# Loads in order of need, and batch 1's attention between group 0's products

## The chip, the core and the metric

The kernel runs on one core of a Trainium2 chip. The metric is the device time of one execution in microseconds (us). All times come from the timed runs of the kernel before and from one profiled execution of it.

## The reference

Sliding-window causal attention (8 batches, 8 heads, 576 positions of 64 values, a window of 64), whose output goes as 4608 tokens of 512 values through a multiplicative feed-forward part:

```python
scores = q @ k.T / 8                     # per batch and head
scores = where(0 <= i - j < 64, scores, -1e9)
attn   = softmax(scores) @ v             # -> x [4608, 512]
h      = ((x @ w1) * (x @ w2)) @ w3      # w1, w2 [512, 1024], w3 [1024, 1024]
out    = h @ w_out                       # w_out [1024, 512], out [4608, 512]
```

## The kernel before

The two last weights are folded once on the chip: `wc = w3 @ w_out` (1024 x 512), in eight parts. `fold_t(fc)` transposes a part of w3 on TensorE and copies it to SBUF, `fold_mm(fc)` multiplies it with w_out, and `fold_step` does the next transposes and one product.

**Attention.** For each batch, `load_qk` brings K and Q in fp32 (1.18 MB each) into a tile `stage`, with positions on partitions; they are cast to fp16 (`cast_third`, a third of the columns at a time, or `cast_qk`, one head of each pair at a time), transposed on TensorE in three groups of six (`transposes(b, which, c)`, with copies out of PSUM into `kT` and `qT`), and then there are six steps `d` per batch (three bands of 192 positions, two halves of the heads). `scores(d)` has TensorE multiply, ACT take the exponential into `pt` (line 279), and POOL mask it (`affine_select`, lines 288 and 290). `values(d)` has TensorE multiply `pt` with V into `o_ps` (line 309), of which there is a single buffer; V carries a block of ones, so that row sums come with it. ACT takes logarithm and exponential of the sums (318, 319, 321), and DVE multiplies (324, 325) into `xT`, the transposed input of the feed-forward part. `load_v` brings a block of V (cast by the DMA), `copy_v` fills the overlaps. `load_qk` may have a gate: a one-column memset on an engine, so that the transfer starts only when that engine's queue has come to this place.

**Feed-forward.** The 4608 tokens are nine groups of 512. `ffn_ab(g, fc)`, a product below, does x @ w1 and x @ w2 for 128 of the 1024 columns (eight matmuls on TensorE, line 395), ACT copies one (400), DVE multiplies (401). `ffn_o(g, t)`, an output product below, multiplies 128 tokens by `wc` (408), DVE copies (410), and `store` sends them out. Group g can start when the attention has filled its 512 columns: group 0 needs batch 0, group 1 needs batch 1's six steps.

**Order.** The kernel sets its order by hand: each engine runs its instructions in the order in which the program writes them, in its own queue. DMAs are issued from the queue of SP (K, Q, stores) and of POOL (V and weights), and an issue is an instruction of that queue, behind everything that stands ahead of it; a queue's ninth transfer waits until its first has landed, and so on. The program is: prologue (batch 0's K and Q, with `keep_busy` matmuls on TensorE that have no use but to be run), six steps of batch 0 with the folds, eight products of group 0, six steps of batch 1 with output products, and from group 1 on a list of `slots` (each a product or an output product) between which `tick(u)` puts the attention of batch 2 and later, by the due times in the loop at the end and the table `late`. `todo` adds batch 2's transposes behind group 1's first slots.

Of the kernel before, what the change touches and what calls it, by code (L numbers as in the profile page):

```python
# [15 lines left out]
P = 128  # L16
# [128 lines left out]
def kernel(  # L145
# [11 lines left out]
    nc = tc.nc  # L157
# [44 lines left out]
    def load_qk(b, which, gate=None):  # L202
        src = k if which == "k" else q
        t = sb.tile([P, 2, TI * D], FP32, name="stage", bufs=4)
        if gate is not None:
            gate(t[:, 0, 0:1], 0.0)
        for j in range(NJ):
            nc.sync.dma_start(out=t[j:P:NJ],
                              in_=src[b, 2 * j:2 * j + 2].rearrange("h (p r) d -> p h (r d)", r=TI))
        raws[which, b] = t  # L210
# [16 lines left out]
    def load_v(b, c):  # L227

        vh = v16s[b % 2].rearrange("p c j (a e) -> p c (j a) e", a=2)[:, :, :, 0:D]
        lo = D if c == 4 else 0  # L230
        s0 = VBLK[c] + lo
        nc.gpsimd.dma_start(out=vh[lo:P, c], in_=v[b, :, s0:s0 + P - lo, :].rearrange("h s d -> s h d"))  # L232

    def copy_v(b, c):
        vh = v16s[b % 2].rearrange("p c j (a e) -> p c (j a) e", a=2)[:, :, :, 0:D]
# [91 lines left out]
    def keep_sums(n):  # L327
# [155 lines left out]
    load_wo()  # L483
    load_w3(0)
    load_w3(1)
# [33 lines left out]
    keep_busy(60)  # L519
# [5 lines left out]
    keep_busy(15)  # L525
# [4 lines left out]
    tps = spare(ps_s, "s_ps")  # L530
    transposes(0, "q", 2, tps[0])
# [68 lines left out]
    for g in range(1, NG):  # L600
# [4 lines left out]
        first = 5 if g == 1 else 0  # L605
# [60 lines left out]
```

## Time and profile before

| | |
|---|---|
| Time, median of 3 runs | 350.1 us (349.34 to 351.72) |
| Profiled execution | 347.68 us, of which the span is 345.9 us |
| Mean granted TensorE clock | 0.918 |
| Busy: TensorE matmul / weight load | 288.4 us (83%) / 168.4 us (49%) |
| Busy: DVE / ACT / POOL | 198.1 us (57%) / 180.2 us (52%) / 178.0 us (51%) |
| Moved by DMA | 38.89 MB, mean 112 GB/s |
| Chain that ended last | TensorE 59%, of it line 395 32% and line 408 16% of the span |

In the profile PE is TensorE's matmuls, PEld its weight loads, DVE the vector engine, ACT the scalar engine, POOL GpSimd, SP the engine that only issues transfers. A row of the timeline gives the start, the time (from the first to the last of its instructions when it holds several), the engine and line, the operation with its tiles, how many, and in brackets the idle time just before with what ended it. Matmuls overlap one another, so a matmul's own duration is longer than its share of the time. A row of a table by stages gives the stretch, and in it the busy time of PE, PEld, DVE, ACT and POOL, the granted clock, the DMA share and the GB/s moved.

### The profile page before, as it was taken

What the parts mean: (1) busy time and instruction counts of PE and PEld (TensorE: products, weight loads), DVE (VectorE), ACT (ScalarE), POOL (GpSimd) and SP (SyncE); (2) the same over time, 40 slices, a digit from 0 to 9 for tenths busy, and PEclk for the clock granted to TensorE, in tenths of its full rate; (3) what the DMA queues carried; (4) which work ended last, traced back from release to release, by engine and by line L of the source; (5) the groups of instructions that cost most, each with busy time, mean ns of one, the idle gap of its engine ahead of it and who ended that gap; (6) DMA issues with size and microseconds to landing.
All of it is one profiled execution on the core that took longest, in us unless ns stands there. A gap on an engine that the chain in (4) does not pass through costs nothing.

```text
span 345.9 us, 5523 instructions
## 1 busy us (share of the span) xinstructions
PE 288.4 (83%) x2007; PEld 168.4 (49%) x2007; DVE 198.1 (57%) x305; ACT 180.2 (52%) x298; POOL 178.0 (51%) x211
## 2 busy tenths in 40 slices
PE   6486955497674977999999999999999999998790
PEld 6363522144332445555555559855555555443230
DVE  4373651156334385677787776757877765554440
ACT  1243741423654244687877876549768866613100
POOL 9258620500759126988887785468776444300000
PEclk9589999599766696999999999999999999999896
DMA  7999706840467950768768767574049011020021
GB/s 161 286 184 203 117 0 224 100 24 0 144 221 152 283 216 0 74 124 270 49 114 270 78 90 235 117 118 63 2 80 114 0 63 61 2 91 33 2 95 39
DMA packets 52182, 38.89 MB, mean 112 GB/s; under 512 B 39296, under 2 KB 42368, under 8 KB 52144
## 3 DMA queue, kind: packets, MB, share of 16 engines
q0 software_dynamic: 41744, 9.96, 31.1%
q1 hardware_dynamic: 10400, 28.47, 23.8%
q8 instruction: 18, 0.29, 0.4%
q14 instruction: 20, 0.16, 0.2%
HBM read 38.80 MB, written 9.44 MB: 139 GB/s over the span
## 4 chain that ended last, share of the span: by engine, by line
PE 59%; DVE 2%; ACT 2%; issue 1%; POOL 1%; DVEq 0%; POOLq 0%; ACTq 0%
PE f_ps L395 32%; PE f_ps L408 16%; PE o_ps L309 4%; PE s_ps L274 4%; PE tp L251 3%; DVE qT L260 1%; ACT qT L260 0%; DVE xT L325 0%; ACT r L321 0%; POOL pt L290 0%; POOL pt L288 0%; ACT ln_s L319 0%; DVE okv L464 0%; DVE chk L461 0%; ACT pt L279 0%
## 5 line engine op out<-in xcount | busy, mean ns | idle before, releaser
L395 PE MATMUL f_ps<-xT,w_sb 128*128 128x512 f16 (+1 forms) x640 | 142.3, 373 | 10.4 <-ACT a_sb L400 8.4
L288 POOL TENSOR_SCALAR_AFFINE_SELECT pt<-pt 128x512 f16<-128x512 f16 (+1 forms) x64 | 52.7, 823 | 82.5 <-ACT pt L279 82.4
L395 PEld LDWEIGHTS <-w_sb 128*128 128x128 f16 x640 | 62.3, 101 | 67.0 <-issue 21.5
L401 DVE TENSOR_TENSOR ab<-f_ps,a_sb 128x512 f16<-128x512 f32 x72 | 49.7, 691 | 35.9 <-PE f_ps L395 26.7
L408 PE MATMUL f_ps<-wc_sb,ab 128*128 128x512 f16 x288 | 69.7, 390 | 0.1
L400 ACT COPY a_sb<-f_ps 128x512 f32<-128x512 f32 x72 | 41.6, 579 | 44.9 <-PE f_ps L395 44.5
L324 DVE TENSOR_TENSOR xT<-o_ps,r 64x384 f16<-64x384 f32 x48 | 26.4, 550 | 57.1 <-ACT r L321 57.1
L279 ACT ACTIVATE pt<-s_ps 128x1024 f16<-128x1024 f32 (+1 forms) x48 | 45.6, 950 | 25.2 <-PE s_ps L274 24.2
L290 POOL TENSOR_SCALAR_AFFINE_SELECT pt<-pt 128x512 f16<-128x512 f16 (+1 forms) x64 | 52.6, 821 | 4.4
L318 ACT ACTIVATE ln_s<-o_ps 64x384 f32<-64x384 f32 x48 | 23.4, 487 | 46.2 <-PE o_ps L309 46.1
L309 PE MATMUL o_ps<-pt,v 128*128 128x128 f16 (+1 forms) x384 | 29.5, 221 | 16.5 <-DVE xT L325 11.8
L408 PEld LDWEIGHTS <-ab 128*128 128x128 f16 x288 | 27.7, 100 | 29.5 <-issue 3.1
L309 PEld LDWEIGHTS <-v 128*128 128x128 f16 x384 | 24.9, 101 | 28.7 <-issue 13.0
L232 POOL DMA_DIRECT2D v<-in_v_dram x40 | 34.4, 867 | 7.0 <-DMA ab<-in_moe_w_out_dram 6.7
L410 DVE COPY t2k<-f_ps 128x512 f32<-128x512 f32 x36 | 24.9, 692 | 12.0 <-PE f_ps L408 11.3
L274 PE MATMUL s_ps<-qT,kT 128*128 128x256 f16 x192 | 28.7, 275 | 3.2 <-DVE qT L260 2.6
L325 DVE TENSOR_TENSOR xT<-o_ps,r 64x384 f16<-64x384 f32 x48 | 26.9, 561 | 0.7
L321 ACT ACTIVATE r<-ln_s 128x384 f32<-128x384 f32 x48 | 25.1, 522 | 1.5
L274 PEld LDWEIGHTS <-kT 128*128 128x128 f16 x192 | 18.2, 101 | 12.9 <-issue 4.0
L260 DVE COPY qT<-tp 64x768 f16<-64x768 f16 x20 | 19.2, 960 | 7.8 <-ACT qT L260 7.6
L319 ACT ACTIVATE ln_s<-o_ps 64x384 f32<-64x384 f32 x48 | 23.2, 482 | 0.6
L255 DVE COPY kT<-tp 128x768 f16<-128x768 f16 x21 | 19.9, 950 | 2.1 <-PE tp L251 2.0
(60 smaller groups left out, 196.3 us busy)
## 6 DMA issues: line engine op xcount, KB each, us to landing
stage<-in_k_dram SPq DMA_DIRECT2D x32, 288.0 KB
stage<-in_q_dram SPq DMA_DIRECT2D x32, 288.0 KB
out_dram<-t2k SPq DMA_DIRECT2D x36, 256.0 KB
v<-in_v_dram POOLq DMA_DIRECT2D x32, 128.0 KB, 4.2
w_sb<-in_moe_w_dram POOLq DMA_DIRECT2D x4, 512.0 KB, 12.9
ab<-in_moe_w_out_dram POOLq DMA_DIRECT2D x1, 1024.0 KB, 15.4
ab<-in_moe_w_dram POOLq DMA_DIRECT2D x2, 512.0 KB, 17.8
xT<-in_moe_w_dram POOLq DMA_DIRECT2D x2, 512.0 KB, 14.4
```

The source lines that it names most:

```text
L232: nc.gpsimd.dma_start(out=vh[lo:P, c], in_=v[b, :, s0:s0 + P - lo, :].rearrange("h s d -> s h d"))
L274: nc.tensor.matmul(s_ps[:, jj, c0:c0 + 2 * n].rearrange("k (a n) -> k a n", a=2), kT[:, 2 * jp + jj, k0:k0 + P], qT[:, 2 * jp + jj, :, q0: ...
L279: nc.scalar.activation(pt[:, :, 0:w], s_ps[:, :, 0:w], AF.Exp, bias=-SHIFT, scale=scale)
L288: nc.gpsimd.affine_select(out=sl, in_=sl, pattern=pat, compare_op=ALU.is_ge, fill=0.0, base=off, channel_multiplier=-1)
L290: nc.gpsimd.affine_select(out=sl, in_=sl, pattern=[[-s, m] for s, m in pat], compare_op=ALU.is_ge, fill=0.0, base=63 - off, channel_multip ...
L309: nc.tensor.matmul(o_ps[:, jj, o0:o0 + n], v16[:, si * 2 + bi, j0 + jj, a * D:a * D + P], pt[:, jj, c0 + a * n:c0 + a * n + n], start=firs ...
L324: nc.vector.tensor_tensor(xs[0:D], o_ps[0:D, :, 0:192], r[0:D], ALU.mult)
L325: nc.vector.tensor_tensor(xs[D:P], o_ps[D:P, :, 192:384], r[D:P], ALU.mult)
L395: nc.tensor.matmul(d[:, f * n + c0:f * n + c1], w[:, dc, (fc + f) * P:(fc + f + 1) * P], xT[:, dc, xc:xc + c1 - c0], start=first, stop=(dc ...
L400: act_cp(a_sb[:, 0:nf * n], a_ps[:, 0:nf * n])
L401: nc.vector.tensor_tensor(ab[:, fc:fc + nf, lo:hi], b_ps[:, 0:nf * n].rearrange("p (f n) -> p f n", f=nf), a_sb[:, 0:nf * n].rearrange("p ...
L408: nc.tensor.matmul(o_ps, ab[:, fc, t * P:t * P + P], wc_sb[:, fc, :], start=(fc == 0), stop=(fc == 7))
```

## The change

K and Q of a batch come in two transfers each (one per head of a pair, 128 partitions) instead of four (32 partitions). In the prologue POOL first clears V's ones, then issues w_out and the first quarter of w3, three V blocks, the rest of w3; the last two V blocks come behind, and the halves of w1 and w2 later, between batch 0's steps, as do V, K and Q of batch 1. The folds are spread over batch 0's six steps, with `scores` two steps ahead instead of one. Group 0's products are spread: three ahead of batch 1's first scores, one more before its second, one in each of the steps 6 to 9; output products stand in and behind the steps 10 and 11. Batch 2's K is transposed between group 0's last output products instead of in `todo`. In `late` V's five blocks come in two bunches.

```diff
     def load_qk(b, which, gate=None):
...
-        for j in range(NJ):
-            nc.sync.dma_start(out=t[j:P:NJ],
-                              in_=src[b, 2 * j:2 * j + 2].rearrange("h (p r) d -> p h (r d)", r=TI))
+        for hh in range(2):
+            nc.sync.dma_start(out=t[:, hh], in_=src[b, hh:H:2].rearrange("j (p r) d -> p j (r d)", r=TI))
...
     late = {0: [("t", 1, "k", 0), ("cast", 1, "q", 0)], 1: [("cast", 1, "q", 1)],
-            2: [("t", 1, "k", 1), ("load", 2, "k")], 3: [("v", 1, 0)],
-            4: [("t", 1, "k", 2), ("v", 1, 2)], 5: [("load", 2, "q"), ("v", 1, 3)],
-            6: [("t", 1, "q", 0), ("v", 1, 4)], 7: [("v", 1, 5), ("cast", 2, "k", 0)],
-            8: [("t", 1, "q", 1)], 9: [("copy", 1, 1), ("cast", 2, "k", 1)],
-            10: [("t", 1, "q", 2)], 11: [("copy", 1, 4)]}
+            2: [("t", 1, "k", 1), ("load", 2, "k")], 4: [("t", 1, "k", 2), ("v", 1, 0, 2, 3)],
+            5: [("load", 2, "q")], 6: [("t", 1, "q", 0), ("v", 1, 4, 5)], 7: [("cast", 2, "k", 0)],
+            8: [("t", 1, "q", 1), ("copy", 1, 4)], 9: [("copy", 1, 1), ("cast", 2, "k", 1)], 10: [("t", 1, "q", 2)]}
...
-    load_wo()
-    load_w3(0)
-    load_w3(1)
...
     ones_of(0)
-    for c in (0, 2, 3):
-        load_v(0, c)
-    load_w3(2)
-    for c in (4, 5):
-        load_v(0, c)
-    load_w3(3)
-    for half in range(2):
-        for i in range(2):
-            load_w12(i, half)
+    load_wo()
+    load_w3(0)
+    load_v(0, 0, 2, 3)
+    for n in range(1, 4):
+        load_w3(n)
     ones_of(1)
+    load_v(0, 4, 5)
...
-    keep_busy(60)
+    keep_busy(75)
...
-    keep_busy(15)
+    keep_busy(10)
...
     keep_busy(10)
+    scores(0)
+    keep_busy(10)
+    scores(1)
+    for i in range(2):
+        load_w12(i, 0)
     w3Ts[0] = fold_t(0)
-    scores(0)
-    w3Ts[1] = fold_t(1)
+    fold_step(0)
+    fold_mm(1, w3Ts.pop(1), dve_cp)
     copy_v(0, 1)
-    fold_mm(0, w3Ts.pop(0), dve_cp)
     for d in range(6):
-        if d < 5:
-            scores(d + 1)
+        if d == 0:
+            w3Ts[2] = fold_t(2)
+        values(d)
+        if d < 4:
+            scores(d + 2)
+        fold_step(d + 2)
+        if d == 0:
+            load_v(1, 0, 2)
+        if d == 1:
+            load_v(1, 3)
+            load_qk(1, "k", nc.vector.memset)
+            load_qk(1, "q")
+        if d == 2:
+            copy_v(0, 4)
+            for i in range(2):
+                load_w12(i, 1)
         if d == 3:
-            copy_v(0, 4)
-        if d < 5:
-            fold_step(d + 1)
-        values(d)
-    fold_step(6)
-    load_qk(1, "k", nc.vector.memset)
-    load_qk(1, "q")
-    fold_step(7)
+            load_v(1, 4)
+        if d == 4:
+            cast_qk(1, "k", 0, dve_cp)
+            cast_qk(1, "k", 1, dve_cp)
+            cast_qk(1, "q", 0, pool_cp)
+            transposes(1, "k", 0)
+    cast_qk(1, "q", 1, dve_cp)
...
-    for c in range(3):
-        cast_third(1, "k", c, act_cp if c != 1 else dve_cp)
-    for c in range(3):
-        cast_third(1, "q", c, act_cp if c != 1 else pool_cp)
-    for c in (0, 2, 3, 4, 5):
-        load_v(1, c)
-    for fc in range(8):
-        ffn_ab(0, fc)
-        if fc in (4, 5, 6):
-            transposes(1, "k", fc - 4)
+    transposes(1, "k", 1)
+    ffn_ab(0, 0)
+    transposes(1, "k", 2)
+    ffn_ab(0, 1)
     tps = spare(ps_v, "o_ps")
     for c in range(3):
         transposes(1, "q", c, tps[c] if c < 2 else None)
+    ffn_ab(0, 2)
+    load_v(1, 5)
+    scores(6)
     copy_v(1, 1)
-    ffn_o(0, 0)
-    scores(6)
...
-    ffn_o(0, 1)
+    ffn_ab(0, 3)
     scores(7)
...
     for d in range(6, 12):
         values(d)
         if d < 10:
             scores(d + 2)
-        if d in (7, 9):
-            ffn_o(0, (d - 3) // 2)
+            ffn_ab(0, d - 2)
+        else:
+            ffn_o(0, d - 10)
             store()
...
+    transposes(2, "k", 0)
+    ffn_o(0, 2)
+    store()
+    transposes(2, "k", 1)
+    ffn_o(0, 3)
+    store()
+    transposes(2, "k", 2)
...
-        first = 5 if g == 1 else 0
+        first = 3 if g == 1 else 0
...
-    todo = {0: [lambda: transposes(2, "k", 0)], 1: [lambda: transposes(2, "k", 1)],
-            2: [lambda: transposes(2, "k", 2), lambda: copy_v(2, 1), lambda: cast_qk(3, "k", 0, pool_cp)],
-            3: [lambda: transposes(2, "q", 0), lambda: cast_qk(3, "k", 1, pool_cp)],
-            4: [lambda: transposes(2, "q", 1), lambda: copy_v(2, 4)], 5: [lambda: transposes(2, "q", 2)]}
+    todo = {0: [lambda: transposes(2, "q", 0), lambda: copy_v(2, 1)],
+            1: [lambda: transposes(2, "q", 1), lambda: copy_v(2, 4), lambda: cast_qk(3, "k", 0, pool_cp)],
+            2: [lambda: transposes(2, "q", 2), lambda: cast_qk(3, "k", 1, pool_cp)]}
```

POOL's queue in the prologue, before (the line numbers are those of each kernel; `ab` holds w_out and half of w3, `xT` the other half for the time of the folds, `w_sb` w1 and w2, `v_0` V of even batches, `v_1` of odd ones):

```order
L433 DMA ab<-in_moe_w_out_dram 128x8x512
L439 DMA ab<-in_moe_w_dram 128x2x1024 x2
L491 MEMSET v_0_85 128x48x64
L232 DMA v_0_85<-in_v_dram 128x8x64 x3
L439 DMA xT<-in_moe_w_dram 128x2x1024
L232 DMA v_0_85<-in_v_dram 64x8x64
L232 DMA v_0_85<-in_v_dram 128x8x64
L439 DMA xT<-in_moe_w_dram 128x2x1024
L429 DMA w_sb<-in_moe_w_dram 128x4x512 x4
L491 MEMSET v_1_86 128x48x64
L288 AFFINE_SELECT pt<-pt 128x2x256
```

The same place after the change, up to the first mask:

```order
L489 MEMSET v_0_85 128x48x64
L434 DMA ab<-in_moe_w_out_dram 128x8x512
L440 DMA ab<-in_moe_w_dram 128x2x1024
L235 DMA v_0_85<-in_v_dram 128x8x64 x3
L440 DMA ab<-in_moe_w_dram 128x2x1024
L440 DMA xT<-in_moe_w_dram 128x2x1024 x2
L489 MEMSET v_1_86 128x48x64
L235 DMA v_0_85<-in_v_dram 64x8x64
L235 DMA v_0_85<-in_v_dram 128x8x64
L291 AFFINE_SELECT pt<-pt 128x2x256
```

The four w1 and w2 transfers have left the place ahead of the first mask, the first memset stands ahead of w_out, and three V blocks stand ahead of all of w3 but its first quarter.

DVE's queue at the end of batch 0's steps, before (`xT` rows are the multiplications of a values step, `k16` and `q16` the casts of batch 1):

```order
L324 TENSOR_TENSOR xT_83<-o_ps_532,r_544 64x2x192
L325 TENSOR_TENSOR xT_83<-o_ps_532,r_544 64x2x192
L324 TENSOR_TENSOR xT_83<-o_ps_548,r_559 64x2x192
L325 TENSOR_TENSOR xT_83<-o_ps_548,r_559 64x2x192
L448 COPY t2k_572<-f_ps_563 128x1024
L455 CAST wc_sb_61<-f_ps_574 128x512
L206 MEMSET stage_584 128x1
L224 CAST k16_608<-stage_584 128x2x6x64
L401 TENSOR_TENSOR ab_621<-f_ps_623,a_sb_632 128x512
```

And after the change, from the multiplications of step 4 on:

```order
L327 TENSOR_TENSOR xT_83<-o_ps_560,r_572 64x2x192
L328 TENSOR_TENSOR xT_83<-o_ps_560,r_572 64x2x192
L449 COPY t2k_585<-f_ps_576 128x1024
L456 CAST wc_sb_61<-f_ps_587 128x512
L216 CAST k16_597<-stage_458 128x18x64 x2
L258 COPY kT_602<-tp_603 128x128x6
L327 TENSOR_TENSOR xT_83<-o_ps_611,r_622 64x2x192
L328 TENSOR_TENSOR xT_83<-o_ps_611,r_622 64x2x192
L216 CAST q16_600<-stage_462 128x18x64
L258 COPY kT_602<-tp_640 128x128x6
L402 TENSOR_TENSOR ab_648<-f_ps_650,a_sb_659 128x512
```

Two wide casts of batch 1's K and a copy of its transposes now stand between the multiplications of step 4 and step 5, and the gate of its load (the memset) has moved out of this place, to step 1.

ACT's queue from the last fold on, before (`a_sb` is the copy of a product, `pt` the exponential of a scores step):

```order
L455 CAST wc_sb_61<-f_ps_595 128x512
L224 CAST k16_608<-stage_584 128x2x6x64 x2
L224 CAST q16_612<-stage_590 128x2x6x64 x2
L400 COPY a_sb_632<-f_ps_622 128x512
L400 COPY a_sb_645<-f_ps_635 128x512
```

And after the change, from the row behind that fold on:

```order
L401 COPY a_sb_659<-f_ps_649 128x512
L401 COPY a_sb_680<-f_ps_670 128x512
L263 COPY qT_1_88<-o_ps_683 64x4x32x6 x2
L263 COPY qT_1_88<-tp_700 64x4x32x6
L401 COPY a_sb_719<-f_ps_709 128x512
L282 ACTIVATE pt_728<-s_ps_723 128x2x384
L401 COPY a_sb_746<-f_ps_736 128x512
L282 ACTIVATE pt_754<-s_ps_749 128x2x384
L321 ACTIVATE ln_s_769<-o_ps_760 64x384
L322 ACTIVATE ln_s_769<-o_ps_760 64x384
L324 ACTIVATE r_772<-ln_s_769 128x384
L282 ACTIVATE pt_781<-s_ps_776 128x1024
```

The casts of batch 1 are gone from ACT's queue, and the copies of the products stand between the scores and values of batch 1 instead of all ahead of them.

More of the change, by code (lines that the diff above doesn't have):

```diff
@@ L225, in cast_third, with v_heads, load_v @@
            t[:, :, 6 * c * D:6 * c * D + 6 * D].rearrange("p hh (i d) -> p hh i d", d=D))
[L227 to L232, printed above, removed]
+    def v_heads(b):
+        return v16s[b % 2].rearrange("p c j (a e) -> p c (j a) e", a=2)[:, :, :, 0:D]
+    def load_v(b, *blocks):
+        vh = v_heads(b)
+        for c in blocks:
+            lo = D if c == 4 else 0
+            s0 = VBLK[c] + lo
+            nc.gpsimd.dma_start(out=vh[lo:P, c], in_=v[b, :, s0:s0 + P - lo, :].rearrange("h s d -> s h d"))
     def copy_v(b, c):
-        vh = v16s[b % 2].rearrange("p c j (a e) -> p c (j a) e", a=2)[:, :, :, 0:D]
+        vh = v_heads(b)
         dve_cp(vh[0:D, c], vh[D:P, c - 1])
@@ L580 @@
             scores(d + 2)
-        if d in (7, 9):
-            ffn_o(0, (d - 3) // 2)
+            ffn_ab(0, d - 2)
+        else:
+            ffn_o(0, d - 10)
             store()
-        if d in (8, 9):
-            cast_qk(2, "k", d - 8, pool_cp)
-            load_v(2, (d - 8) * 2)
+        if d == 7:
+            copy_v(1, 4)
+            load_qk(2, "k", nc.gpsimd.memset)
+            load_qk(2, "q")
+            load_v(2, 0, 2, 3)
+        if d == 9:
+            load_v(2, 4, 5)
+    cast_qk(2, "k", 0, pool_cp)
+    cast_qk(2, "k", 1, pool_cp)
+    transposes(2, "k", 0)
[5 more added lines that the diff above has]
+    transposes(2, "k", 2)
     cast_qk(2, "q", 0, pool_cp)
```

13 lines of the change are left out of this document (1 added, 12 removed).

## The prediction

> **What bounds the kernel now.** I read the page's 40 slices first, then busy time by stage, then the timeline of the first 135 us engine by engine, where each row ends with the idle time before it and what ended it.
>
> ```profile
> PE   6486955497674977999999999999999999998790
> PEclk9589999599766696999999999999999999999896
> 160.00:310.00 150.00, 149.95 (x1099) 89.96 (x1098) 105.05 (x164) 103.49 (x176) 93.33 (x109) 1.00 0.48 94
> ```
>
> A slice is 8.65 us. From slice 18 on TensorE is full, and the stage row says the same: 149.95 of 150 us busy at clock 1.00 between 160 and 310 us. The change leaves that work there, so nothing is to be won in it; its new order of V loads only has to keep it fed. The time to win lies before about 135 us, where the PE digits are 4 to 9 and the granted clock falls to 5 to 7 tenths. That part runs in four stages, and I take a marker for each: V0 (the second half of batch 0's first values step), S (group 0's first product), N (group 1's first product), T (batch 2's first scores). After T both kernels have the same work left, but for two products of 1.73 us.
>
> **Stage 1, start to V0.** The rows of the load and of POOL's queue:
>
> ```profile
> 0.81 2.74 SPq L208 DMA_DIRECT2D stage<-in_k_dram  x4
> 12.14 0.83 ACT L224 CAST k<-stage 128x768 f16<-128x768 f32 x1 [10.05 <-DMA stage<-in_k_dram]
> 16.69 0.83 ACT L224 CAST q<-stage 128x768 f16<-128x768 f32 x1 [0.39 <-DMA stage<-in_q_dram]
> 17.23 1.27 POOL L232 DMA_DIRECT2D v<-in_v_dram  x1 [6.67 <-DMA ab<-in_moe_w_out_dram]
> 19.70 0.70 POOL L439 DMA_DIRECT2D xT<-in_moe_w_dram  x1 [1.20 <-DMA ab<-in_moe_w_dram]
> 22.19 0.78 POOL L429 DMA_DIRECT2D w_sb<-in_moe_w_dram  x1 [1.80 <-DMA ab<-in_moe_w_dram]
> 23.66 2.34 POOL L429 DMA_DIRECT2D w_sb<-in_moe_w_dram  x3 [0.69 <-DMA v<-in_v_dram]
> 22.20 0.49 PE L274 MATMUL s_ps<-qT,kT 128*128 128x256 f16 x4
> 25.98 2.68 POOL L491 MEMSET v<- 128x3072 f16 x1
> 30.87 0.44 PE L309 MATMUL o_ps<-pt,v 128*128 128x64 f16 x7 [0.65 <-POOL pt L290]
> 54.00:62.00 8.00, 2.69 (x13) 1.10 (x12) 0.56 (x1) 2.15 (x3) 0.00 (x0) 0.89 0.88 296
> ```
>
> K is there at 12.1 and Q at 16.7 us, because w_out and w3 flow beside them; the last row (54 to 62 us, batch 1's K and Q with nothing beside them) shows 296 GB/s, the last column. Scores follow Q by 5.5 us (22.20). Then the masks of L288 and L290 wait for POOL, which first waits for landings, issues four w1/w2 transfers and clears v (25.98 to 28.66). V0 is 30.87.
>
> After the change, K (1.18 MB at 296 GB/s: 4.0 us) starts at about 2.2, where data begins today, and is usable at 7.7 with 1.5 us for its end to be seen. POOL clears v first (2.7 us), so w_out's data starts near 6 and shares with Q; Q comes at 12 to 15, scores at 18 to 20. From 6 us on, 1.26 MB of K and Q and 1.05 MB of w_out are left: 7.8 us at 296 GB/s, so w_out lands at 14 to 17 (17.2 today, less at most what K has gained). Behind it in POOL's queue, by the distances between the landings above: w3's first quarter 2.5 us (17.2 to 19.7), V about 1.5 a block for three (22.2 to 23.7, 3.5 in all as they overlap), w3's second quarter 2.5. That quarter is there at 22.5 to 25.5, and its transposes stand ahead of values(0) on TensorE. POOL is free earlier: its last wait is for w3's first quarter, 17 to 19.5, then 0.9 for an issue and 2.1 for the first masks. **V0 falls from 30.87 to about 25.0**: 5.9 us. The longer warm-up (75 matmuls for 60) runs while K is awaited, at 5.5 us per 60 it ends at 8.3, 0.6 after K at most.
>
> **Stage 2, V0 to S.**
>
> ```profile
> 34.19 0.50 PE L309 MATMUL o_ps<-pt,v 128*128 128x128 f16 x8 [0.27 <-DVE xT L325]
> 48.08 0.61 PE L309 MATMUL o_ps<-pt,v 128*128 128x128 f16 x8 [2.88 <-DVE xT L325]
> 53.94 2.75 PE L395 MATMUL f_ps<-xT,w_sb 128*128 128x512 f16 x12
> 17.00 1.02 DVE L224 CAST q<-stage 128x768 f16<-128x768 f32 x2
> 103.06 1.13 POOL L217 CAST k<-stage 128x1152 f16<-128x1152 f32 x1
> ```
>
> A values step waits for DVE to empty its PSUM tile: 30.87 to 34.19 is 3.3 us, five steps to 48.08 are 17.2. I take 3.4 a step. Today S is 53.94, 23.1 us after V0, with the last two folds behind the loop. After, the folds are inside the loop, but batch 1's K is cast on DVE ahead of its transposes, and these stand ahead of values(5). The wide cast on DVE is not in the trace: at least one of the two narrow ones (0.5), at most POOL's 1.13; I take 0.8, nearer to DVE's own row (1.5 times the columns). Two are 1.6. DVE gets to them at V0 + 18.6 (43.6, after values(4)'s multiplications, a copy and a cast), so values(5) comes at 45.7, its multiplications end 3.3 later: **S = 49.0**, 4.9 us earlier than 53.94, if K is there by 43.6 and Q by 49.
>
> Is it? Their gate on DVE opens in step 1 after its multiplications, at V0 + 7.7 = 32.7.
>
> ```profile
> 52.79 2.53 SPq L208 DMA_DIRECT2D stage<-in_k_dram  x4
> 59.93 1.56 ACT L224 CAST k<-stage 128x768 f16<-128x768 f32 x2 [5.21 <-DMA stage<-in_k_dram]
> 63.03 1.56 ACT L224 CAST q<-stage 128x768 f16<-128x768 f32 x2 [1.53 <-DMA stage<-in_q_dram]
> 65.13 5.28 PE L395 MATMUL f_ps<-xT,w_sb 128*128 128x512 f16 x12 [8.44 <-ACT a_sb L400]
> ```
>
> Today K comes 7.1 and Q 10.2 us after the first issue: 39.8 and 42.9 if alone. Beside them run the first halves of w1 and w2, three V blocks and then the second halves. At half the rate (4.0 more for each) they come at 43.8 and 50.9: at most 0.2 us late for K and 1.9 for Q. I count none and keep the 2 us in the range. [...]
>
> **Stage 3, S to N.** Here is the main gain. ACT's in-order queue holds the casts of batch 1 ahead of the copies of the products, and TensorE stands 8.44 us (above) before it goes on at half clock.
>
> ```profile
> 79.97 0.50 PE L251 MATMUL o_ps<-ident,q 128*128 128x128 f16 x6
> 85.61 0.49 PE L274 MATMUL s_ps<-qT,kT 128*128 128x256 f16 x4 [0.70 <-DVE qT L260]
> 89.33 0.45 PE L309 MATMUL o_ps<-pt,v 128*128 128x64 f16 x7 [0.65 <-POOL stage L206]
> 108.88 1.01 PE L309 MATMUL o_ps<-pt,v 128*128 128x128 f16 x8 [2.88 <-DVE xT L325]
> 112.67 2.72 PE L395 MATMUL f_ps<-xT,w_sb 128*128 128x512 f16 x6 [1.93 <-DVE xT L325]
> 157.27 1.73 PE f_ps L395 x8
> 163.89 0.33 PE tp L251 x6
> ```
>
> Today eight products, Q's transposes, the scores' chain and six values steps stand one behind the other: 112.67 - 53.94 = 58.7 us. After, counted from S: product 0, K's last transposes and product 1 take 1.73 + 0.34 + 1.73 = 3.8; from Q's transposes to scores(6) 5.64 (79.97 to 85.61; product 2 lies inside); to values(6) 3.72 (85.61 to 89.33; product 3 inside): 13.2. Five steps of 3.4 reach values(11) at 30.2: a step holds values, scores and one product, 0.45 + 0.45 + 1.73 = 2.6 us of TensorE, less than the chain through ACT and DVE. Behind it 0.45, three output products (5.2) and three K transposes (1.0) cover the 3.8 us that N waits today: **36.9 us instead of 58.7**, 21.8 less.
>
> **Stage 4, N to T.**
>
> ```profile
> 113.00:118.00 5.00, 5.00 (x18) 2.15 (x17) 1.56 (x2) 0.81 (x2) 0.94 (x2) 0.50 1.39 313
> 122.87 0.50 PE L251 MATMUL tp<-ident,q 128*128 128x128 f16 x6
> 125.90 0.49 PE L251 MATMUL tp<-ident,q 128*128 128x128 f16 x6 [0.80 <-DVE qT L260]
> 128.28 0.49 PE L251 MATMUL tp<-ident,q 128*128 128x128 f16 x6 [0.16 <-DVE qT L260]
> 130.67 0.49 PE L274 MATMUL s_ps<-qT,kT 128*128 128x256 f16 x4 [1.89 <-DVE qT L260]
> ```
>
> Today 18.0 us with six products, five of the first at clock 0.50 and three K transposes. After: one product (1.73), then the same chain from 122.87 to 130.67 (7.8), during which three more products run: 9.5. The two missing products cost 3.5 later: 13.0, **5.0 less**.
>
> **The sum.** 4.9 + 21.8 + 5.0 = 31.7 us. The profiled execution has 347.68 (span 345.9 and 1.8 around it), so 316.0. The three timed runs have their median 2.4 above it; with these 2.4 the forecast is **318 us** against 350.1.
>
> **Where it may go otherwise.**
>
> (a) Batch 1's loads come late. At a third of the rate K lands at 47.8 and Q at 58.9: DVE stands up to 4 us in step 4 and 6 more before the copies of S. 318 + 10 = 328. For it: the weights and V of the first 40 us now share the DMA engines with 2.4 MB more. Against: w1 and w2's second halves start later. 10%.
>
> (b) The woven steps are longer, since ACT's copy and DVE's product enter the chain.
>
> ```profile
> L401 DVE TENSOR_TENSOR ab<-f_ps,a_sb 128x512 f16<-128x512 f32 x72 | 49.7, 691 | 35.9 <-PE f_ps L395 26.7
> L400 ACT COPY a_sb<-f_ps 128x512 f32<-128x512 f32 x72 | 41.6, 579 | 44.9 <-PE f_ps L395 44.5
> ```
>
> With both in full a step is 3.4 + 0.58 + 0.69 = 4.7, four such steps add 5: 323. They stand behind the values in both queues, which speaks against. 9%.
>
> (c) The clock falls in stage 3.
>
> ```profile
> 92.00:97.00 5.00, 4.35 (x19) 2.24 (x20) 1.62 (x3) 2.67 (x5) 3.23 (x3) 0.50 0.89 278
> 41.00:49.00 8.00, 4.84 (x53) 3.41 (x54) 5.79 (x9) 4.17 (x8) 4.19 (x4) 1.00 0.00 0
> ```
>
> From 92 to 97 us it was 0.50 after a stand of 2.4 us; from 41 to 49 it stayed at 1.00 over one of 2.88 (row of 48.08). At half clock a step's 2.6 us become 5.2, 1.8 more than the chain; six steps add 11: 329. The new stage has stands of under 1 us in its steps and 2 in Q's chain, so 5%. [...]
>
> (d) Slower than before: two transfers of 128 partitions may move K and Q more slowly than four of 32. No such load is in the trace. At rate r K takes 1180/r us, with r in GB/s. At 80, Q lands at 33 and V0 moves to 42.4 (+17); batch 1's K comes 7 after its place and Q 9 after that: 33 us, all of the gain. Below about 80 GB/s it decides; at 60 the same steps give +53, so 371. The bytes and the queue are those of the 296 GB/s row: 4%.
>
> (e) The order is new but the waits only move on, to K of batch 2 or 3 or to POOL's masks, and T comes back to where it was: 350. The room that POOL has in stage 3 (2.2 us of masks per 3.4) speaks against: 2%.
>
> **How the numbers follow.** The forecast's own case has 70%: unknowns of 2.5 on V0, 2 on Q, 2 on the steps and 1 on the casts give 311 to 323. (b), (a) and (c) lie at 323, 328 and 329; with these the range is 309 to 330. One per cent, 3.5 us, is about what a measurement of this kernel tells from no change. (a), (b), (c) and the own case are all faster: 94%; (e) with its 2% is the same; (d) is slower, 4%.
>
> **What would show it.** K's first cast near 8 us and Q's near 13; V0 near 25; no stand of 8 us before the products; S near 49; values steps of 3.4 us with one product between; N near 86, T near 95; after that TensorE full as before; PEclk digits of 9 from slice 3 on. Wrong would be: K cast later than 12 us (d), a DVE stand before the wide K casts of over 2 us (a), steps over 4 us (b), or a new gap of TensorE after T.

## The result, and the profile after

The changed kernel takes **318.84 us** (median of 4 runs, 316.18 to 320.36) against 349.72 us (348.12 to 351.72) for the kernel before on the same chip: a ratio of **0.911 [0.903, 0.919]**. The profiled execution has 317.97 us, span 316.2, mean granted clock 0.965 (0.918 before). Here and below a ratio is estimated from the fast runs of both kernels, so it can differ a little from the quotient of the two medians.

The page after: TensorE's busy tenths and granted clock in 40 slices of 7.9 us, and the stage row of the part that was full before (its columns as above).

```profile
PE   8578959677897999999999999999999999996880
PEclk9869997999999799999999999999999999999796
130.00:280.00 150.00, 149.22 (x1095) 89.63 (x1094) 106.93 (x165) 103.84 (x176) 93.58 (x109) 1.00 0.46 93
```

TensorE's digit stays at 9 from slice 13 on (103 us); before, the same digit stood from slice 16 on (138 us), a little ahead of the slice 18 that the prediction took. The full part is the same: 149.22 of 150 us at clock 1.00. Of the slices ahead of it seven have a PE digit below 8, where there were twelve, and PEclk falls to 6 or 7 at three places (slices 2, 6 and 13, the last of them just behind T).

The timeline after, engine by engine, at the markers:

```profile
6.54 0.83 ACT L223 CAST k<-stage 128x768 f16<-128x768 f32 x1 [4.45 <-DMA stage<-in_k_dram]
10.53 2.71 POOL L489 MEMSET v<- 128x3072 f16 x1
11.60 2.52 DVE L223 CAST q<-stage 128x768 f16<-128x768 f32 x2
13.72 0.67 PE L254 MATMUL o_ps<-ident,q 128*128 128x128 f16 x6 [2.47 <-DVE q L223]
16.00:18.00 2.00, 0.85 (x9) 0.85 (x9) 1.97 (x3) 0.62 (x1) 0.70 (x1) 0.50 1.77 173
18.17 0.84 PE L277 MATMUL s_ps<-qT,kT 128*128 128x256 f16 x4
27.08 0.46 PE L312 MATMUL o_ps<-pt,v 128*128 128x64 f16 x7 [0.92 <-DVE v L241]
44.07 1.16 POOL L216 CAST q<-stage 128x1152 f16<-128x1152 f32 x1
45.37 1.80 DVE L216 CAST k<-stage 128x1152 f16<-128x1152 f32 x2
47.23 0.51 PE L254 MATMUL tp<-ident,k 128*128 128x128 f16 x6 [3.77 <-DVE k L216]
47.58 0.61 PE L312 MATMUL o_ps<-pt,v 128*128 128x128 f16 x8
48.00:50.00 2.00, 2.00 (x9) 0.72 (x7) 0.94 (x2) 1.49 (x3) 0.00 (x0) 0.51 1.62 184
51.77 1.89 PE L396 MATMUL f_ps<-xT,w_sb 128*128 128x512 f16 x8
64.93 0.45 PE L312 MATMUL o_ps<-pt,v 128*128 128x64 f16 x7 [0.65 <-POOL pt L293]
68.25 0.50 PE L312 MATMUL o_ps<-pt,v 128*128 128x128 f16 x8 [0.71 <-DVE xT L328]
71.63 0.61 PE L312 MATMUL o_ps<-pt,v 128*128 128x128 f16 x8 [0.71 <-DVE xT L328]
89.61 1.89 PE L396 MATMUL f_ps<-xT,w_sb 128*128 128x512 f16 x8
98.49 0.49 PE L277 MATMUL s_ps<-qT,kT 128*128 128x256 f16 x4 [0.16 <-DVE qT L263]
104.00:106.00 2.00, 2.00 (x7) 0.77 (x6) 1.11 (x2) 0.83 (x2) 1.93 (x4) 0.50 0.32 129
```

V0 is the row at 27.08, S at 51.77, N at 89.61, T at 98.49. In stage 3 a values step takes 3.3 to 3.7 us (the first at 64.93, 68.25 and 71.63) with a product inside, and its own wait in these rows is 0.71 us. The sum of the two traces, in us:

| | before | after | gain | forecast |
|---|---|---|---|---|
| start to V0 | 30.87 | 27.08 | 3.8 | 5.9 |
| V0 to S | 23.07 | 24.69 | -1.6 | -1.0 |
| S to N | 58.73 | 37.84 | 20.9 | 21.8 |
| N to T, and two products that come later (3.46) | 18.00 | 8.88 + 3.46 | 5.7 | 5.0 |
| T to the end, less these 3.46 | 215.2 | 214.2 | 1.0 | 0 |
| span | 345.9 | 316.2 | 29.7 | 31.7 |

### The profile page after: what moved, and what is told of

It is laid out like the page before. It is cut to its first block, busy times and chain, and to the rows that moved or that the text cites. A ratio compares the mean times of both kernels' runs of the same rounds, so it can differ in the third digit from the quotient of the medians.

```text
span 316.2 us, 5497 instructions
## 1 busy us (share of the span) xinstructions
PE 280.5 (89%) x2027; PEld 165.4 (52%) x2027; DVE 201.9 (64%) x307; ACT 176.8 (56%) x294; POOL 179.1 (57%) x211
## 4 chain that ended last, share of the span: by engine, by line
PE 73%; DVE 9%; ACT 7%; issue 4%; POOL 4%; DVEq 0%; POOLq 0%; ACTq 0%
PE f_ps L396 33%; PE f_ps L409 18%; PE o_ps L312 6%; PE s_ps L277 5%; PE tp L254 4%; PE tp L477 3%; DVE qT L263 2%; PE f_ps L455 2%; POOL pt L291 2%; ACT ln_s L322 2%; ACT qT L263 2%; ACT r L324 2%; DVE xT L328 1%; POOL pt L293 1%; ACT pt L282 1%
## 5 line engine op out<-in xcount | busy, mean ns | idle before, releaser
L396 PE MATMUL f_ps<-xT,w_sb 128*128 128x512 f16 (+1 forms) x640 | 137.5, 364 | 0.7 <-DVE ab L402 0.7
L396 PEld LDWEIGHTS <-w_sb 128*128 128x128 f16 x640 | 60.9, 99 | 52.2 <-issue 4.6
L409 PE MATMUL f_ps<-wc_sb,ab 128*128 128x512 f16 x288 | 67.1, 379 | 0.1
L402 DVE TENSOR_TENSOR ab<-f_ps,a_sb 128x512 f16<-128x512 f32 x72 | 49.7, 691 | 24.1 <-PE f_ps L396 20.1
L409 PEld LDWEIGHTS <-ab 128*128 128x128 f16 x288 | 27.0, 98 | 27.6 <-issue 0.3
L312 PE MATMUL o_ps<-pt,v 128*128 128x128 f16 (+1 forms) x384 | 28.0, 215 | 8.2 <-DVE xT L328 4.3
L312 PEld LDWEIGHTS <-v 128*128 128x128 f16 x384 | 23.6, 98 | 20.8 <-issue 6.6
L277 PE MATMUL s_ps<-qT,kT 128*128 128x256 f16 x192 | 27.9, 269 | 1.5 <-DVE qT L263 0.9
## 6 DMA issues: line engine op xcount, KB each, us to landing
stage<-in_k_dram SPq DMA_DIRECT2D x16, 576.0 KB
stage<-in_q_dram SPq DMA_DIRECT2D x16, 576.0 KB
```

What stands on the lines that cost most here:

```text
L277: nc.tensor.matmul(s_ps[:, jj, c0:c0 + 2 * n].rearrange("k (a n) -> k a n", a=2), kT[:, 2 * jp + jj, k0:k0 + P], qT[:, 2 * jp + jj, :, q0: ...
L312: nc.tensor.matmul(o_ps[:, jj, o0:o0 + n], v16[:, si * 2 + bi, j0 + jj, a * D:a * D + P], pt[:, jj, c0 + a * n:c0 + a * n + n], start=firs ...
L396: nc.tensor.matmul(d[:, f * n + c0:f * n + c1], w[:, dc, (fc + f) * P:(fc + f + 1) * P], xT[:, dc, xc:xc + c1 - c0], start=first, stop=(dc ...
L402: nc.vector.tensor_tensor(ab[:, fc:fc + nf, lo:hi], b_ps[:, 0:nf * n].rearrange("p (f n) -> p f n", f=nf), a_sb[:, 0:nf * n].rearrange("p ...
L409: nc.tensor.matmul(o_ps, ab[:, fc, t * P:t * P + P], wc_sb[:, fc, :], start=(fc == 0), stop=(fc == 7))
```

## The experiments

The kernels ran in three groups, each with the kernel before beside it: experiments 1 to 4 (before: 347.33 us); experiments 5 to 7 and the changed kernel (346.72); experiments 8 and 9 and the kernel of 7 once more (348.33). Ratios are to the kernel before of the same group. Marker times are of one profiled run each.

### 1. Four transfers of 32 partitions again

```diff
-        for hh in range(2):
-            nc.sync.dma_start(out=t[:, hh], in_=src[b, hh:H:2].rearrange("j (p r) d -> p j (r d)", r=TI))
+        for j in range(NJ):
+            nc.sync.dma_start(out=t[j:P:NJ],
+                              in_=src[b, 2 * j:2 * j + 2].rearrange("h (p r) d -> p h (r d)", r=TI))
```

> The changed kernel with K and Q in four transfers of 32 partitions again, all else as changed. Theory A (the form of the transfer does not matter, as the prediction had it): 318.8, within 1 us of the changed kernel; K cast near 6.5 us, Q near 11. Theory B (two transfers of 128 partitions move faster: the changed kernel's trace has 406 GB/s from 4 to 8 us and 397 from 94 to 104, the one before 296 from 54 to 62): K cast at 7.5 to 8, Q at 13 to 14, the rate of batch 3's load near 300, V0 1 to 2 us later, 320 to 322 in all.

Measured: 322.4 us, ratio 0.932 [0.925, 0.939], against 0.911 and (in the second group) 0.913 of the changed kernel. Stage rows of the loads of batch 0, 1 and 2 (last column GB/s, all queues together), first of the changed kernel:

```profile
4.00:8.00 4.00, 4.00 (x48) 4.00 (x47) 3.13 (x4) 0.83 (x1) 4.00 (x5) 1.00 1.01 406
38.00:42.00 4.00, 3.82 (x37) 2.37 (x36) 3.04 (x6) 2.98 (x6) 3.93 (x5) 1.00 1.02 371
94.00:104.00 10.00, 7.90 (x58) 4.26 (x56) 6.49 (x9) 5.66 (x9) 6.19 (x8) 0.93 1.01 397
```

and of this one, with its K casts on DVE and the clearing of V on POOL beside them:

```profile
4.00:8.00 4.00, 4.00 (x53) 3.94 (x51) 2.19 (x3) 0.47 (x1) 4.00 (x5) 1.00 0.91 260
38.00:44.00 6.00, 5.47 (x53) 3.71 (x53) 3.52 (x8) 4.44 (x9) 5.85 (x6) 1.00 1.12 180
96.00:106.00 10.00, 8.61 (x63) 4.71 (x62) 7.47 (x11) 5.79 (x8) 3.54 (x5) 1.00 0.88 293
7.55 6.23 DVE L224 CAST k<-stage 128x768 f16<-128x768 f32 x2 [1.53 <-DMA stage<-in_k_dram]
10.33 3.03 POOL L490 MEMSET v<- 128x3072 f16 x1
31.67 0.46 PE L313 MATMUL o_ps<-pt,v 128*128 128x64 f16 x7 [0.92 <-DVE v L242]
```

The four-transfer form moves the same bytes more slowly (in the first and last window 260 and 293 GB/s for 406 and 397), which is the opposite of the rival with slower transfers. But of the 4.6 us by which V0 is later, the landing of K is only 1.0 (7.53 for 6.54): the two casts that follow took 6.23 us for 1.40. The second of them began at 10.7, within POOL's clearing of V (10.33 to 13.36), and ended 0.42 us after it; the first took 3.2 us beside POOL's transfer issues, which no run explains, since in the changed kernel the pair took 1.40 beside such issues. T is 4.7 us later (103.16). The price of the old form is thus 3 to 7 us here, the smaller by the spans (319.1 and 316.2), the larger by the ratios, and part of it is that stall. The spans understate it: the changed kernel's trace has a stretch of half clock behind T (104 us) that this one lacks.

### 2. Group 0's products not woven

The loads and batch 0's steps as changed; in stage 3 the order of before: eight products, then Q's transposes, then batch 1's six steps with two output products between.

```diff
-    ffn_ab(0, 0)
-    transposes(1, "k", 2)
-    ffn_ab(0, 1)
+    for fc in range(8):
+        ffn_ab(0, fc)
+        if fc == 4:
+            transposes(1, "k", 2)
...
-            ffn_ab(0, d - 2)
```

> The changed kernel with stage 3 in the order of before: eight products of group 0, then Q's transposes, batch 1's six steps with four output products among them; early loads, front and casts as changed. Theory (weaving hides the products under the chain of the values steps): from the first product to group 1's first product 47 to 50 us instead of 37.8, in all 328 to 331. Rival (the gain of stage 3 was the stand of 8.4 us for batch 1's casts and the half clock behind it, which the early load alone removes): less than 4 us lost, 319 to 323.

Measured: 330.63 us, ratio 0.952 [0.945, 0.958]. S and N in its timeline:

```profile
51.55 8.80 PE L396 MATMUL f_ps<-xT,w_sb 128*128 128x512 f16 x40
68.08 0.49 PE L254 MATMUL o_ps<-ident,q 128*128 128x128 f16 x6 [1.89 <-DVE qT L263]
95.32 0.82 PE L254 MATMUL tp<-ident,k 128*128 128x128 f16 x6 [1.33 <-POOL k L216]
100.20 2.91 PE L396 MATMUL f_ps<-xT,w_sb 128*128 128x512 f16 x8
```

S is where it was (51.55), S to N is 48.65 us. So the 20.9 us of stage 3 have two halves: 58.73 to 48.65, 10.1 us, came from the casts that had left ACT's queue and loads that were there (the stand of 8.44 us is gone, five products run in one row of 8.80), and 48.65 to 37.84, 10.8 us, from the weaving. The border is not sharp: the three transposes of batch 2's K stand behind the last values step here (95.32, then 97.76 and 99.61, with waits of 1.33, 1.62 and 1.05 us), while in before they came after N and in the changed kernel they lie between output products. So the first half is at least 10.1 us, and the second holds the hiding of these transposes too.

### 3. Batch 1's K and Q loaded behind batch 0's steps

The casts of batch 1 and its first transposes stand behind these loads.

```diff
             load_v(1, 3)
-            load_qk(1, "k", nc.vector.memset)
-            load_qk(1, "q")
...
+    load_qk(1, "k", nc.vector.memset)
+    load_qk(1, "q")
```

> The changed kernel with batch 1's K and Q issued behind batch 0's six steps and cast there, woven order kept. Theory: values(5) comes 3.5 us earlier since no cast stands ahead of it, but TensorE then stands about 8 to 10 us for K and Q and its clock falls: 5 to 9 us lost, 324 to 328. Rival (an early load only moves the wait, since DVE, not the DMA, sets K's casts): within 2 us of the changed kernel, 317 to 321.

Measured: 322.64 us, ratio 0.930 [0.924, 0.936].

```profile
53.55 0.82 PE L254 MATMUL tp<-ident,k 128*128 128x128 f16 x6 [7.28 <-DVE k L216]
56.02 2.34 PE L396 MATMUL f_ps<-xT,w_sb 128*128 128x512 f16 x5
```

TensorE stands 7.28 us for K where the changed kernel stands 3.77, and S comes at 56.02 instead of 51.77. The early load is worth 4 to 7 us (S 4.3, span 4.7, T 6.6, ratios 6 to 7), not a whole stand of 7 to 8 with the half clock behind it, because the early casts cost a stand of their own.

### 4. POOL's old order in the prologue

w_out and w3's first half ahead of the clearing of V, all of w1 and w2 and the second clearing ahead of the first masks, as before; the rest as changed.

```diff
+    load_wo()
+    load_w3(0)
+    load_w3(1)
...
     ones_of(0)
-    load_wo()
-    load_w3(0)
     load_v(0, 0, 2, 3)
...
+    for half in range(2):
+        for i in range(2):
+            load_w12(i, half)
+    ones_of(1)
```

> The changed kernel with POOL's issues in the order of before (w_out and half of w3 first, V and w3, all of w1 and w2, then the second memset), all else as changed. Theory of the prediction (K and Q alone on the DMA engines and POOL free for the masks bring V0 from 30.9 to 27): V0 at 30 to 32, 4 to 5 us lost, 322 to 324. Rival (V0 is set by the chain behind Q's casts, which cost 2.06 us each beside POOL's memset in the changed kernel, so the old order gives some of it back): V0 at 27 to 29, 318 to 320.

Measured: 321.79 us, ratio 0.926 [0.919, 0.933].

```profile
12.51 0.83 ACT L223 CAST q<-stage 128x768 f16<-128x768 f32 x1 [2.16 <-DMA stage<-in_q_dram]
25.24 2.69 POOL L492 MEMSET v<- 128x3072 f16 x1
30.18 0.69 PE L312 MATMUL o_ps<-pt,v 128*128 128x64 f16 x7 [0.60 <-POOL pt L293]
```

K lands as early as in the changed kernel and Q only 1.4 us later, yet V0 is 30.18: the masks wait for POOL, which clears V at 25.24. In this prologue it is POOL's queue, not the landing of K and Q, that set V0 before, and its order is worth 3.1 us there.

### 5. The second clearing of V behind batch 0's scores

```diff
-    ones_of(1)
     load_v(0, 4, 5)
...
         load_w12(i, 0)
+    ones_of(1)
     w3Ts[0] = fold_t(0)
-    fold_step(0)
-    fold_mm(1, w3Ts.pop(1), dve_cp)
-    copy_v(0, 1)
+    w3Ts[1] = fold_t(1)
+    copy_v(0, 1)
+    fold_mm(0, w3Ts.pop(0), dve_cp)
+    fold_mm(1, w3Ts.pop(1), dve_cp)
```

> The changed kernel with POOL's second memset moved behind the first two w1/w2 issues (from 10.5 us to about 24), and the two V copies on DVE ahead of the first fold products. Theory (a DVE cast from SBUF to SBUF stands while POOL's memset runs: 2.06 us instead of 0.55 in the changed kernel): Q's two DVE casts take 0.55 each, first scores at 16 to 17 instead of 18.2, V0 at 24.5 to 25.5 instead of 27.1, 1.5 to 2.5 us gained. Rival (V0 is set by landings of w3 and V): Q's casts shorter, V0 within 0.7 us of 27.1.

Measured: 315.24 us, ratio 0.912 [0.904, 0.919]; the changed kernel, run beside it, 316.69 us, 0.913 [0.907, 0.920].

> The changed kernel itself, beside the next three on one chip, as their reference. Every theory: its ratio to the kernel before stays at 0.91, and its stages stay within 1 us (batch 0's first values step complete at 27, first product at 52, group 1's first product at 90, batch 2's first scores at 98 to 99).

```profile
11.69 1.02 DVE L223 CAST q<-stage 128x768 f16<-128x768 f32 x2
16.45 0.49 PE L277 MATMUL s_ps<-qT,kT 128*128 128x256 f16 x4 [0.16 <-DVE qT L263]
16.00:18.00 2.00, 1.50 (x23) 1.23 (x20) 0.39 (x1) 0.81 (x1) 0.70 (x1) 1.00 1.86 169
23.51 0.62 PE L447 MATMUL f_ps<-ident,ab 128*128 128x128 f16 x8 [0.23 <-DMA ab<-in_moe_w_dram]
23.97 0.50 PE L312 MATMUL o_ps<-pt,v 128*128 128x128 f16 x8
```

With nothing on POOL beside them, the two casts of Q take 1.02 us instead of 2.52, the clock stays at 1.00, the copies of V are no longer late, and V0 falls from 27.1 to 24.1. The edit does two things, and no run parts them: it moves the clearing, and it puts the copies of V ahead of the fold's casts on DVE. The trace parts them roughly, as the first scores, which stand ahead of the copies, are 1.7 us earlier (16.45 for 18.17), and the other 1.3 us come behind them. What it meets there is the load that I had named: TensorE waits 0.23 us for w3's second quarter at 23.51. S, N and T are 2.5 us earlier (49.24, 87.08, 95.97). The medians show 1.5 of it, less than their scatter (313.65 to 316.87 and 315.57 to 318.48), so the mechanism is shown by the trace, and its worth in time only roughly.

### 6. Batch 1's first K cast on ACT, its transposes behind the loop

```diff
         if d == 4:
-            cast_qk(1, "k", 0, dve_cp)
+            cast_qk(1, "k", 0, act_cp)
             cast_qk(1, "k", 1, dve_cp)
             cast_qk(1, "q", 0, pool_cp)
-            transposes(1, "k", 0)
-    cast_qk(1, "q", 1, dve_cp)
+    cast_qk(1, "q", 1, act_cp)
+    transposes(1, "k", 0)
```

> The changed kernel with one of the two K casts and the last Q cast of batch 1 on ACT, and K's first transposes behind the last fold instead of ahead of values(5). Theory (TensorE stands 3.8 us in step 4 for DVE's place in order, not for the landing, since POOL's cast of Q had landed data at 42.9): no stand ahead of values(5), which comes at 44.1 instead of 47.6; first product at 47.5 to 49 instead of 51.8; 3 to 4 us gained. Rival (K lands only just before 45): ACT stands for K and holds values(5)'s logarithms, less than 1 us gained.

Measured: 313.9 us, ratio 0.906 [0.899, 0.913], 2.8 us under the changed kernel.

```profile
46.40 0.50 PE L254 MATMUL tp<-ident,k 128*128 128x128 f16 x6
48.74 1.89 PE L396 MATMUL f_ps<-xT,w_sb 128*128 128x512 f16 x8
```

The stand of 3.77 us is gone (the transposes at 46.40 wait for nothing), S is at 48.74, 3.0 us earlier, and so are N and T (86.58, 95.46). This is the same K, loaded at the same time, and ACT casts its first half at 42.64 without a wait: the stand was DVE's queue, not the landing.

### 7. Both, and transposes and products in turn at the head of stage 3

With the edits of 5 and 6, which are not shown again:

```diff
-    transposes(1, "k", 1)
+    transposes(1, "k", 1, spare(ps_s, "s_ps")[0])
     ffn_ab(0, 0)
     transposes(1, "k", 2)
-    ffn_ab(0, 1)
-    tps = spare(ps_v, "o_ps")
-    for c in range(3):
-        transposes(1, "q", c, tps[c] if c < 2 else None)
+    transposes(1, "q", 0, spare(ps_v, "o_ps")[0])
+    ffn_ab(0, 1)
+    transposes(1, "q", 1, spare(ps_s, "s_ps")[0])
+    transposes(1, "q", 2)
     ffn_ab(0, 2)
```

> Both edits of the two kernels above, and Q's first transposes of batch 1 ahead of product 1, with PSUM tiles of their own for three of the six groups of transposes. Theory: V0 at 25, first product at 45 to 47, and from there to group 1's first product 35.5 to 37 instead of 37.8, since the chain of Q's copies starts a product earlier: 6 to 8 us less than the changed kernel. Rival (the copies of the transposes queue on DVE behind the products' multiplications): 3 to 5 us less.

Measured: **309.27 us, ratio 0.891 [0.883, 0.899]**, 7.4 us under the changed kernel beside it; run again in the last group 307.77 us, 0.883 [0.878, 0.888].

> The same kernel as e8_better, run beside the next one as its yardstick: 305 to 311 us, S at 44.7, T at 89.8.

```profile
44.95 1.89 PE L396 MATMUL f_ps<-xT,w_sb 128*128 128x512 f16 x8
80.76 1.89 PE L396 MATMUL f_ps<-xT,w_sb 128*128 128x512 f16 x8
90.23 0.49 PE L277 MATMUL s_ps<-qT,kT 128*128 128x256 f16 x4 [0.75 <-DVE qT L263]
```

These are S, N and T of the second run: 6.8, 8.9 and 8.3 us earlier than in the changed kernel. This version beats both kernels. The turns at the head of stage 3 were not run alone; what the two edits before gave apart (1.5 and 2.8) leaves about 3 us for them.

### 8. The kernel before with the new transfers alone

```diff
-        for j in range(NJ):
-            nc.sync.dma_start(out=t[j:P:NJ],
-                              in_=src[b, 2 * j:2 * j + 2].rearrange("h (p r) d -> p h (r d)", r=TI))
+        for hh in range(2):
+            nc.sync.dma_start(out=t[:, hh], in_=src[b, hh:H:2].rearrange("j (p r) d -> p j (r d)", r=TI))
```

> The kernel before with one function changed: each load of K or Q is two transfers of 128 partitions and 196 KB in place of four of 32 partitions. Order of loads and of work are those of before. Theory (the form itself is faster): where batch 1's K and Q load, at 54 to 62 us, the GB/s column rises from 296 to 370 or more, the stand for K at the head of stage 3 (8.4 us in before) shortens by a quarter to a third, and the time is 2 to 5 us under before's. Rival (the form is only faster where nothing else loads): the rate stays within 5% of 296 and the time within 1.5 us of before's.

(The 196 KB there is a slip of mine: the page lists 576.0 KB for each of the two transfers and 288.0 KB for each of the four.) Measured: 344.73 us, ratio 0.991 [0.987, 0.995]. First before's rows of batch 1's load, then this kernel's, with the first cast of batch 0's K and Q and the stand:

```profile
54.00:58.00 4.00, 2.69 (x13) 1.10 (x12) 0.00 (x0) 0.59 (x1) 0.00 (x0) 1.00 0.91 278
58.00:62.00 4.00, 0.00 (x0) 0.00 (x0) 0.56 (x1) 1.56 (x2) 0.00 (x0) 0.78 0.85 315
```

```profile
58.00:62.00 4.00, 0.34 (x2) 0.06 (x1) 0.56 (x1) 1.56 (x2) 0.00 (x0) 1.00 1.00 368
6.45 0.83 ACT L223 CAST k<-stage 128x768 f16<-128x768 f32 x1 [4.36 <-DMA stage<-in_k_dram]
12.68 0.83 ACT L223 CAST q<-stage 128x768 f16<-128x768 f32 x1 [2.56 <-DMA stage<-in_q_dram]
65.63 4.56 PE L394 MATMUL f_ps<-xT,w_sb 128*128 128x512 f16 x12 [7.28 <-ACT a_sb L399]
```

With nothing else loading the rate goes from 278 to 315 up to 368 GB/s: the form itself is faster. Batch 0's K is there at 6.45 for 12.14 and Q at 12.68 for 16.69, in before's order of POOL's loads. Little comes of it: V0 moves by 0.8 us only (30.06), as POOL's masks set it (experiment 4), and the stand for batch 1 shrinks by 1.2 us, 14% and not the quarter to a third that I expected. In all it is 3.6 us by the medians and 2.1 by the spans (343.8 for 345.9). Not all of it can be followed: S is 1.65 us later than in before (55.59), behind a stretch of low clock (0.54 from 28 to 32 us, 0.60 from 32 to 36), while N and T are 1.5 and 1.3 earlier (111.17, 129.36). In the changed kernel the same form is worth 3 to 7 us, part of it the stall of experiment 1; that fewer other waits hide it there is a guess.

### 9. Batch 2's pieces apart

On the kernel of experiment 7:

```diff
-            slots.append((w, lo + (hi - lo) * share + (LAG + 1) * (i >= first)))
+            lag = min(LAG + 1, 1.2 * (i + 1 - first)) if g == 1 else LAG + 1
+            slots.append((w, lo + (hi - lo) * share + lag * (i >= first)))
```

> e8_better with one rule of the planner changed: in group 1 the pieces of batch 2 that fall due at once at T (scores and transposes that stand back to back without a product between them) become due one after the other, 1.2 us apart. Theory (the idle of about 3 us between T and the next product, and the clock of 0.50 for 2 to 3 us behind it, come from pieces bunched at one place): the next product follows T within 1 us, the clock stays at 1.00, and the time is 2 to 4 us under e8_again's. Rival (the attention chain through ACT and POOL sets the pace there whatever the order): the idle moves to the next products, and the time is within 1 us of e8_again's.

Measured: 307.97 us, ratio 0.883 [0.879, 0.888], against 307.77 beside it: no difference, the rival's case.

```profile
91.16 1.89 PE L396 MATMUL f_ps<-xT,w_sb 128*128 128x512 f16 x8
97.72 0.22 PE L312 MATMUL o_ps<-pt,v 128*128 128x128 f16 x1 [0.55 <-POOL pt L293]
98.58 0.44 PE L312 MATMUL o_ps<-pt,v 128*128 128x64 f16 x7 [0.65 <-POOL pt L293]
94.00:104.00 10.00, 8.58 (x70) 5.22 (x70) 6.14 (x9) 7.70 (x14) 9.79 (x13) 1.00 0.52 129
```

The product now follows T (90.50) at once, but the idle time has moved to the values steps behind, which wait for POOL's masks; POOL is busy 9.79 of these 10 us, and 9.79 too in the kernel without the edit. That POOL sets the pace there fits these waits; no run with less work on POOL shows it. A part of my theory was wrong from the start: the half clock behind T, which the profiled run of experiment 7 had, is absent from the second run of the same kernel.

## Why the prediction was right, point by point

The forecast of 318 us, the gain of 31.7 and its place (stage 3) came out: 318.84, 29.7 by the spans, 20.9 of it from S to N. That the time is met within 1 us is partly luck: the gain was 2.0 us too high, and the 2.4 us added for the distance of the median from the profiled run, which is 0.9 here (318.84 and 317.97), were 1.5 too many, and the two errors cancel but for 0.5. The steps:

**K and Q early: right, better than forecast, and for half the reason.** First casts at 6.54 and 11.10 us, for 7.7 and 12 to 15. The 1.5 us for the end of K's load was an estimate: of the 7.1 us from issue to cast of batch 1's K in before, 4.0 for its bytes and 1.4 ahead of them (as for batch 0, 0.81 to 2.2) leave 1.7; Q's last bytes moved by 62.3 us, and its cast began at 63.03, 0.7 later. The rate of 296 GB/s was that of the old form; from 4 to 8 us the new one showed 406 and the old one, in experiment 1, 260. I had K late in before because w_out and w3 flow beside it. They still do in experiment 8, and K is there at 6.45, with 320 GB/s from 4 to 8 us for 195 in before; with the new order and the old form (experiment 1) it is there at 7.53. So either edit alone brings 4.6 to 5.7 us of K's 5.6, and the form, which I had counted at nothing, brings as much as the order. Rival (d), the only one on the slower side, is refuted by experiments 1 and 8: the two-transfer form is the faster one.

**V0 = 25.0: 2.1 us too early, and the step that failed is its limit.** I let the landing of w3's second quarter limit it. What limited it was the chain behind Q's casts: scores came 7.1 us after the first of them (11.10 to 18.17) and not 5.5, and between scores and the first values matmul (25.94) TensorE's own order holds the second scores and two folds, 7.8 us that my sum did not have. One of the casts took 2.06 us for 0.54 (one, not each, as I wrote for experiment 4), because POOL clears V at that moment; TensorE's wait of 2.47 us for it was followed by clock 0.50 from 14 to 20 us, and then DVE's casts of the fold stood ahead of the copies of V (0.92 us at 27.08). Experiment 5 takes the clearing away, puts the copies first and finds V0 at 24.1, with a wait of 0.23 us for the w3 that I had named.

**V0 to S = 24.0: 24.7 measured.** The two wide casts (1.80 us for my 1.6) and the distance from V0 to values(5) (20.5 for 20.7) are as worked out, K was there in time, and values steps of 3.4 held. The stand that these casts make, 3.77 us on TensorE, lies inside the 20.5. Missing was the low clock behind it, 0.51 in the row at 48 us: from values(5) to S it took 4.2 us (47.58 to 51.77) for 3.3. Rival (a), late loads, did not happen: the casts show no wait for a transfer, and experiment 6 removes the stand without touching a load. POOL casts the first half of Q at 44.07, 9.65 us after the first issue (34.42), and waits for nothing. Half the rate for these loads was an assumption of mine, which no run shows: by it K and half of Q, 1.77 MB, would need an estimated 8.7 us at half of 406 GB/s and some 2.8 around it (batch 0's K: 5.73 from its issue at 0.81 to its cast, 2.9 of it at 406 GB/s), so 11.5. They came sooner, and the 2 us were not paid. All queues together moved 371 GB/s from 38 to 42 us; what part of that K and Q had is not shown.

**S to N = 36.9: 37.84 measured.** Steps of 3.3 to 3.7 us with a product in each; rival (b), 4.7 us a step, and rival (c), a clock that falls in stage 3, did not happen: the clock is 1.00 from 52 us to N. Experiment 2 sizes the weaving at 10.8 of the 20.9 us, the hiding of batch 2's K transposes included.

**N to T: 8.9 for 9.5; after T: 1.0 gained, for 0.** Rival (e) is out: T did not come back to where it was. One of my signs failed, the PEclk digits of 9 from slice 3 on: slices 6 and 13 show 7. The second is the row at 104 us, clock 0.50 behind T, as before had it behind its T (0.50 from 133 to 136). From T to the end it took 217.4 to 217.7 us in the five traces that have this stretch (here and in experiments 2, 4, 6 and the first run of 7) and 215.8 to 217.1 in five that do not (experiments 1, 3 and 5 and the second runs of the changed kernel and of 7).

The gain was forecast 2.1, 0.6 and 0.9 us too high in the first three stages and 0.7 and 1.0 too low in the last two. So loads that were faster than I counted on (368 GB/s with nothing beside them, for 296) worked against stalls around DVE's casts that I had not priced.

## What to carry to other kernels

Where several engines' in-order queues feed one another, look for the product that stands behind other work in a *copying* engine's queue: putting the products between the steps of an attention chain, and its casts elsewhere on data that had been loaded earlier, gave 20.9 of 29.7 us without removing any work. When a load is moved forward, look next at what its first consumer meets on its own engine at the new time: here both remaining stalls (experiments 5 and 6) were casts, not transfers. And a faster transfer pays only as far as the queue behind it is free: alone it brought K's first cast forward by 5.7 us and V0 by 0.8.

## What the runs showed of the hardware

- The same bytes over the same queue moved at 368 GB/s in two transfers over all 128 partitions (experiment 8, 58 to 62 us) and at 278 to 315 in four that each touch every fourth partition (before, 54 to 62 us), with nothing beside them; the DMA share of those rows is 1.00 for 0.85 to 0.91. Why is not shown.
- A DVE cast between two SBUF tiles took longer beside POOL's clearing of V, which had begun before it. In the changed kernel a cast that began at 11.60 took 2.06 us (the other of the pair 0.54) and ended at 13.66, 0.42 after the clearing (10.53 to 13.24); in experiment 1 one that began at 10.7 took 3.1 us and ended 0.42 after its own (13.36). With the clearing moved (experiment 5) the pair took 1.02. Why is not shown.
- In the changed kernel the clock fell to 0.50 behind the wait of 2.47 us (14 to 20 us) and to 0.51 behind that of 3.77 (48 to 50). In these runs the length of the last wait alone did not decide it. Over a wait of 2.88 us it stayed at 1.00 in before (48.08) and was 0.60 behind the same wait in experiment 8 (49.33; 48 to 52 us). Around a wait of 2.09 us in the prologue it fell to 0.50 in one run of the kernel of experiment 7 (16 to 18 us) and stayed at 1.00 in the other (14 to 20 us). Behind T it fell to 0.50 in the changed kernel (row at 104 us) and stayed at 1.00 in its second run (100 to 108 us), with no single wait over 0.65 us there in either. So its fall could not be foretold from one trace.
